# Feature projections of a linear-attention kernel as pairs of 64-row matmuls, one head on each half of the TensorE array

## The chip, the cores and the metric

The kernel runs on one core of one Trainium2 chip. The metric is the device time of one execution in microseconds. Three runs of the kernel before gave a median of 502.53 us (502.03 to 510.46).

## The reference

Eight batches of eight heads go through a linear attention, and its output through a gated convolution. Cut to what matters:

```python
def phi(x):                                   # x: (batch, head, 576, 64); w_phi: (64, 128)
    proj = np.einsum('bhsd,df->bhsf', x, w_phi)
    proj = proj - np.max(np.abs(proj), axis=-1, keepdims=True)
    return np.concatenate([np.exp(proj), np.exp(-proj)], axis=-1)
q_p, k_p = phi(q), phi(k)
kv  = np.einsum('bhsf,bhsd->bhfd', k_p, v)
num = np.einsum('bhsf,bhfd->bhsd', q_p, kv)
den = np.einsum('bhsf,bhf->bhs', q_p, k_p.sum(axis=2))[..., None] + 1e-6
x   = num / den                               # heads side by side: (batch, 576, 512)
proj = x @ w_proj                             # x1, x2, x3 of 512 columns each
y = x1 * irfft(rfft(x2) * rfft(filter)) * x3
out = y @ w_out
```

## The kernel before

**Tiles.** A batch has 576 positions, cut in five chunks of 128 (the last one has 64 real rows). Heads are worked in pairs, four pairs to a batch. For a pair, q and k are transposed on TensorE (L256, copied by ScalarE at L258 to qT and kT) so that rows 0 to 63 hold the 64 dimensions of one head and rows 64 to 127 those of the other. The weight tile wpp is 128 x 256: w_phi stands in rows 0 to 63, columns 0 to 127, and again in rows 64 to 127, columns 128 to 255; the rest is zero. One matmul over all 128 rows so projects both heads at once, and half of its products are with zeros.

**Three projection groups per pair.** `pk_group` projects k: four matmuls of 256 columns into Pk_m (two PSUM banks; chunks 0 and 1 in one, 2 and 3 in the other) and one into Pk_t for the last chunk (L272). ScalarE takes exp and exp of the negative from them (Epk, Emk, L274 to L277), VectorE the largest absolute value (mxk, L278, L281); from that come em and mxe, with which POOL (GpSimd) multiplies v (v1, v2, L292 and L296). `pqt_group` projects q with positions along the columns: two matmuls of 512 columns into Pq_m (L313), one head and one bank each, and two of 128 into Pq_t (L316); ScalarE makes Eq and Eqm (L319 to L322). `pqn_group` projects q again like k, for its largest absolute value alone (Pqn_m, Pqn_t, L335; mxq, L337, L340).

**The rest of a pair.** `kv_group` sums features times v into KV (L355); `nem_group` and `nep_group` multiply the q features with it (L373, L392), VectorE combines them (tmp L379, NEt L397), takes the reciprocal (r, L399) and writes x_nat (L404). `xt_group` transposes x_nat (xtr, L411; copied to xT at L414).

**The gated convolution of a batch** then works on xT: x2 (L598), a discrete Fourier transform as matmuls (L613), the spectrum's products on VectorE, x1 (L540) and x3 (L568), the inverse transform (L656, tail L675; the products yT at L661 and, for the tail, L680), and the last projection (L689), whose accumulator VectorE copies to o (L694), which SyncE's queue stores to memory (L695). Two o buffers alternate.

**Loads.** `load_stage` issues the loads of q, k and v of the next batch on POOL's queue, five for each tensor (L240), and four memsets on VectorE: the ones column of the v tile (L243) and the padding rows of the v, q and k tiles (L244 to L246). The memset of the ones column waits for all five loads of v, since they write the same tile.

**Order.** For each batch `merge_weighted` merges the groups of the attention of batch i with those of the convolution of batch i-1. The framework then schedules: it gives each engine its own order of instructions from the dependencies and from what it expects each instruction to take. On an engine instructions run strictly in that order. PSUM is shared by tags: "proj" has two buffers of two banks (Pk_m, Pq_m, Pqn_m, NEm, NEp), "b1" four buffers of one bank (accumulators, tails, transposes, KV).

Of the kernel before, what the change touches and what calls it, by code (L numbers as in the profile page):

```python
# [13 lines left out]
AF = mybir.ActivationFunctionType  # L14
# [3 lines left out]
PART = 128  # L18
SEQ = 576
HDIM = 64  # L20
# [3 lines left out]
NFEAT = 128  # L24
# [33 lines left out]
def psum_proj(pools, shape, name):  # L58
    return pools["psum"].tile(shape, FP32, name=name, tag="proj", bufs=PROJ_BUFS)


def psum_b1(pools, shape, dtype, name):
    return pools["psum"].tile(shape, dtype, name=name, tag="b1", bufs=B1_BUFS)
# [195 lines left out]
    return dst  # L259


def pk_group(nc, pools, cdict, st, hp, v_stage):
    wpp = cdict["wpp"]
    kT = st["kT"][hp]
    Epk = pools["attn"].tile([PART, 5, 2 * NFEAT], BF16, name="Epk", tag="Epk")
    Emk = pools["attn"].tile([PART, 5, 2 * NFEAT], BF16, name="Emk", tag="Emk")
    mxk = pools["attn"].tile([PART, 5, 2], FP32, name="mxk", tag="mxk")
    Pk_m = psum_proj(pools, [PART, 4, 2 * NFEAT], "Pk_m")
    Pk_t = psum_b1(pools, [PART, 2 * NFEAT], FP32, "Pk_t")
    for (ci, s0, rows) in s_chunks():  # L270
        dst = Pk_m[:, ci, :] if ci < 4 else Pk_t
        nc.tensor.matmul(dst, lhsT=kT[:, s0:s0 + PART], rhs=wpp,  # L272
                         start=True, stop=True)
    nc.scalar.activation(Epk[:, 0:4, :], Pk_m, AF.Exp, bias=0.0, scale=1.0)  # L274
    nc.scalar.activation(Epk[:, 4, :], Pk_t, AF.Exp, bias=0.0, scale=1.0)
    nc.scalar.activation(Emk[:, 0:4, :], Pk_m, AF.Exp, bias=0.0, scale=-1.0)  # L276
    nc.scalar.activation(Emk[:, 4, :], Pk_t, AF.Exp, bias=0.0, scale=-1.0)  # L277
    nc.vector.tensor_reduce(out=mxk[:, 0:4, :],  # L278
                            in_=Pk_m.rearrange("p c (h f) -> p c h f", h=2),
                            axis=AX.X, op=ALU.max, apply_absolute_value=True)  # L280
# [14 lines left out]
    v2 = pools["attn"].tile([PART, 2, 5, HDIM + 1], BF16, name="v2", tag="v2")  # L295
    nc.gpsimd.tensor_tensor(out=v2, in0=vsl,  # L296
                            in1=mxer.to_broadcast([PART, 2, 5, HDIM + 1]),
                            op=ALU.mult)
    st["Epk"][hp] = Epk
    st["Emk"][hp] = Emk  # L300
    st["v1"][hp] = v1
    st["v2"][hp] = v2


def pqt_group(nc, pools, cdict, st, hp):
    wpp = cdict["wpp"]
    qT = st["qT"][hp]
    Eq = pools["attn"].tile([PART, 2, 640], BF16, name="Eq", tag="Eq", bufs=3)
    Eqm = pools["attn"].tile([PART, 2, 640], BF16, name="Eqm", tag="Eqm", bufs=3)
    Pq_m = psum_proj(pools, [PART, 2, 512], "Pq_m")  # L310
    Pq_t = psum_b1(pools, [PART, 2, PART], FP32, "Pq_t")
    for j in range(2):
        nc.tensor.matmul(Pq_m[:, j, :],  # L313
                         lhsT=wpp[:, j * NFEAT:(j + 1) * NFEAT],
                         rhs=qT[:, 0:512], start=True, stop=True)
        nc.tensor.matmul(Pq_t[:, j, :],  # L316
                         lhsT=wpp[:, j * NFEAT:(j + 1) * NFEAT],
                         rhs=qT[:, 512:640], start=True, stop=True)
    nc.scalar.activation(Eq[:, :, 0:512], Pq_m, AF.Exp, bias=0.0, scale=1.0)  # L319
    nc.scalar.activation(Eq[:, :, 512:640], Pq_t, AF.Exp, bias=0.0, scale=1.0)  # L320
    nc.scalar.activation(Eqm[:, :, 0:512], Pq_m, AF.Exp, bias=0.0, scale=-1.0)  # L321
    nc.scalar.activation(Eqm[:, :, 512:640], Pq_t, AF.Exp, bias=0.0, scale=-1.0)  # L322
    st["Eq"][hp] = Eq
    st["Eqm"][hp] = Eqm


def pqn_group(nc, pools, cdict, st, hp):
    wpp = cdict["wpp"]
    qT = st["qT"][hp]
    mxq = pools["attn"].tile([PART, 5, 2], FP32, name="mxq", tag="mxq")  # L330
    Pqn_m = psum_proj(pools, [PART, 4, 2 * NFEAT], "Pqn_m")
    Pqn_t = psum_b1(pools, [PART, 2 * NFEAT], FP32, "Pqn_t")
    for (ci, s0, rows) in s_chunks():
        dst = Pqn_m[:, ci, :] if ci < 4 else Pqn_t
        nc.tensor.matmul(dst, lhsT=qT[:, s0:s0 + PART], rhs=wpp,  # L335
                         start=True, stop=True)
    nc.vector.tensor_reduce(out=mxq[:, 0:4, :],  # L337
                            in_=Pqn_m.rearrange("p c (h f) -> p c h f", h=2),
                            axis=AX.X, op=ALU.max, apply_absolute_value=True)
# [78 lines left out]
def attn_stream_groups(nc, pools, cdict, b, stages, st):  # L418
# [27 lines left out]
    def g_pk(hp):  # L446
        def f():
            pk_group(nc, pools, cdict, st, hp, v_stage)
        return f

    def g_pqt(hp):
        def f():
            pqt_group(nc, pools, cdict, st, hp)
        return f

    def g_pqn(hp):
        def f():
            pqn_group(nc, pools, cdict, st, hp)
        return f
# [395 lines left out]
```

## Time and profile before

| | |
|---|---|
| median of three runs | 502.53 us (502.03 to 510.46) |
| span of the profiled execution | 505.9 us |
| mean granted TensorE clock in it | 0.927 |
| TensorE matmuls busy | 402.8 us (80%), 3672 recorded |
| TensorE weight loads busy | 240.8 us (48%), 3734 |
| VectorE busy | 357.6 us (71%) |
| ScalarE busy | 307.3 us (61%) |
| POOL busy | 200.3 us (40%) |

The profiled execution is one of its own, beside the three timed ones; the page gives its span, from the first to the last instruction, and no other time of it. Matmul busy times overlap, since matmuls are pipelined and a row of 0.38 us can start 0.22 us after the one before it; what a matmul costs in a stream is the distance of starts. Some matmul records are missing, so a group that issues 128 may show fewer. The chain of work that ended last goes back from the last instruction to what released it, and so on; its shares say which engines and waits set the end. In a timeline row the first number is the start, the second the duration, both in microseconds, and the bracket at the end gives the engine's idle time before the row and what ended it. A row with xN merges N instructions.

### The profile page before, as it was taken

How to read it: one execution, taken by the hardware profiler on the slowest of the kernel's cores; microseconds unless marked ns; L12 is line 12 of the kernel's file. 1: busy time of each engine (PE TensorE's matmuls, PEld its weight loads, DVE VectorE, ACT ScalarE, POOL GpSimd, SP SyncE). 2: the span in 40 equal slices, each digit the busy share in tenths (PEclk: the TensorE clock that was granted, in tenths of full speed). 3: DMA queues.
4: the chain of work that ended last, by engine and by line, in shares of the span. 5: the costliest groups of instructions: out<-in, count | busy, mean ns of one | idle time of the engine just before them, and what ended most of it. 6: DMA issues, size and time to landing. Idle time of an engine off the chain costs nothing.

```text
span 505.9 us, 9253 instructions
## 1 busy us (share of the span) xinstructions
PE 402.8 (80%) x3672; PEld 240.8 (48%) x3734; DVE 357.6 (71%) x546; ACT 307.3 (61%) x611; POOL 200.3 (40%) x212
## 2 busy tenths in 40 slices
PE   1566559988688796879798795888888898889995
PEld 0344435555355553545455463554545554555442
DVE  2267654497567884697859785697777986798664
ACT  1669858877079633985189352994279636963220
POOL 9789921158012860346312760246512211221000
PEclk9856659999899998998999798998999999999999
DMA  9999970059610893039900796019910011001102
GB/s 84 176 144 95 95 47 1 0 33 78 75 54 1 53 94 89 2 21 75 124 19 1 50 75 113 1 11 74 99 53 2 2 43 53 0 2 43 53 1 95
DMA packets 119724, 26.92 MB, mean 53 GB/s; under 512 B 113472, under 2 KB 114560, under 8 KB 119680
## 3 DMA queue, kind: packets, MB, share of 16 engines
q0 software_dynamic: 114432, 16.88, 47.4%
q1 hardware_dynamic: 5248, 9.44, 5.4%
q8 instruction: 29, 0.48, 0.4%
q14 instruction: 15, 0.12, 0.1%
HBM read 33.75 MB, written 9.44 MB: 85 GB/s over the span
## 4 chain that ended last, share of the span: by engine, by line
PE 48%; DVE 20%; ACT 15%; DMA 6%; POOL 6%; issue 5%; DVEq 0%; POOLq 0%; ACTq 0%
PE acc L598 7%; PE acc L656 7%; PE acc L568 6%; DVE x_nat L404 5%; PE acc L613 5%; DMA out_dram<-o 4%; ACT Epk L274 3%; PE acc L689 3%; ACT Emk L276 3%; PE trp L256 3%; DVE mxk L278 2%; PE xtr L411 2%; PE acc L540 2%; PE KV L355 2%; DVE NEt L397 2%
## 5 line engine op out<-in xcount | busy, mean ns | idle before, releaser
L414 ACT COPY xT<-xtr 128x640 bf16<-128x640 bf16 x32 | 22.5, 702 | 78.6 <-PE xtr L411 78.6
L278 DVE TENSOR_REDUCE mxk<-Pk_m 128x8 f32<-128x1024 f32 x32 | 39.1, 1221 | 41.8 <-ACT Emk L276 41.7
L337 DVE TENSOR_REDUCE mxq<-Pqn_m 128x8 f32<-128x1024 f32 x32 | 39.0, 1218 | 14.7 <-PE Pqn_m L335 14.4
L411 PE MATMUL xtr<-ident,x_nat 128*128 128x128 bf16 x160 | 16.3, 240 | 39.9 <-DVE x_nat L404 39.9
L598 PE MATMUL acc<-wproj_sb,xT 128*128 128x512 bf16 x153 | 44.3, 411 | 3.6 <-ACT qT L258 3.3
L240 POOL DMA_DIRECT2D qs<-in_q_dram x40 | 34.5, 874 | 27.4 <-PE trp L256 20.1
L274 ACT ACTIVATE Epk<-Pk_m 128x1024 bf16<-128x1024 f32 x32 | 32.7, 1022 | 19.2 <-PE Pk_m L272 19.2
L689 PE MATMUL acc<-wout_sb,yT 128*128 128x512 bf16 x146 | 39.8, 388 | 3.4 <-DVE yT L661 2.5
L602 DVE CAST x2n<-acc 128x512 bf16<-128x512 f32 (+1 forms) x40 | 26.9, 687 | 20.2 <-PE acc L598 20.1
L694 DVE COPY o<-acc 128x512 f32<-128x512 f32 (+1 forms) x40 | 27.2, 679 | 18.9 <-DMA out_dram<-o 9.4
L240 POOL DMA_DIRECT2D ks<-in_k_dram x40 | 33.9, 878 | 10.1 <-PE trp L256 10.1
L404 DVE TENSOR_TENSOR x_nat<-NEt,r 128x640 bf16<-128x640 f32 x32 | 35.6, 1111 | 0.6
L319 ACT ACTIVATE Eq<-Pq_m 128x1024 bf16<-128x1024 f32 x32 | 34.1, 1065 | 2.9 <-PE Pq_m L313 2.9
L568 PE MATMUL acc<-xT,wproj_sb 128*128 128x512 bf16 x120 | 35.3, 421 | 0.4
L240 POOL DMA_DIRECT2D vs<-in_v_dram x40 | 34.1, 881 | 2.8 <-POOL v_518 L296 0.6
L321 ACT ACTIVATE Eqm<-Pq_m 128x1024 bf16<-128x1024 f32 x32 | 33.8, 1058 | 0.0
L411 PEld LDWEIGHTS <-x_nat 128*128 128x128 bf16 x160 | 10.9, 106 | 48.0 <-DVE x_nat L404 46.1
L540 PE MATMUL acc<-xT,wproj_sb 128*128 128x512 bf16 x121 | 31.4, 378 | 2.7 <-ACT x1s L544 2.4
L613 PE MATMUL acc<-x2n,fwdS 128*128 128x512 bf16 x117 | 29.1, 378 | 5.3 <-ACT Cxs L617 5.0
L276 ACT ACTIVATE Emk<-Pk_m 128x1024 bf16<-128x1024 f32 x32 | 33.1, 1033 | 0.0
L661 DVE TENSOR_TENSOR yT<-acc,ts 128x512 bf16<-128x512 f32 x32 | 22.0, 688 | 12.8 <-PE acc L656 7.8
L572 DVE TENSOR_TENSOR ts<-acc,x1s 128x512 bf16<-128x512 f32 x32 | 22.0, 690 | 12.1 <-PE acc L568 10.0
(315 smaller groups left out, 1066.0 us busy)
## 6 DMA issues: line engine op xcount, KB each, us to landing
out_dram<-o SPq DMA_DIRECT2D x32, 256.0 KB, 2.0
qs<-in_q_dram POOLq DMA_DIRECT2D x32, 128.0 KB, 4.1
ks<-in_k_dram POOLq DMA_DIRECT2D x32, 128.0 KB, 4.5
vs<-in_v_dram POOLq DMA_DIRECT2D x32, 128.0 KB, 4.8
wproj_sb<-in_moe_w_proj_dram POOLq DMA_DIRECT2D x4, 384.0 KB, 8.3
out_dram<-o SPq DMA_DIRECT2D x8, 128.0 KB, 2.2
qs<-in_q_dram POOLq DMA_DIRECT2D x8, 64.0 KB, 3.9
ks<-in_k_dram POOLq DMA_DIRECT2D x8, 64.0 KB, 4.2
```

Of the source, the lines that this page charges most:

```text
L240: nc.gpsimd.dma_start(out=dst[0:rows, ci, :, 0:HDIM], in_=src[b, :, s0:s0 + rows, :].rearrange("h p d -> p h d"))
L274: nc.scalar.activation(Epk[:, 0:4, :], Pk_m, AF.Exp, bias=0.0, scale=1.0)
L276: nc.scalar.activation(Emk[:, 0:4, :], Pk_m, AF.Exp, bias=0.0, scale=-1.0)
L278: nc.vector.tensor_reduce(out=mxk[:, 0:4, :], in_=Pk_m.rearrange("p c (h f) -> p c h f", h=2), axis=AX.X, op=ALU.max, apply_absolute_value ...
L337: nc.vector.tensor_reduce(out=mxq[:, 0:4, :], in_=Pqn_m.rearrange("p c (h f) -> p c h f", h=2), axis=AX.X, op=ALU.max, apply_absolute_valu ...
L404: nc.vector.tensor_tensor(out=out_view, in0=num_view, in1=r_b, op=ALU.mult)
L411: nc.tensor.transpose(trp[:, ci, :], x_nat[:, ci, t * PART:(t + 1) * PART], ident)
L540: nc.tensor.matmul(acc, lhsT=wproj[:, kt, m * PART:(m + 1) * PART], rhs=xT_sb[:, kt, 0:512], start=(kt == 0), stop=(kt == 3))
L568: nc.tensor.matmul(acc, lhsT=wproj[:, kt, 1024 + m * PART:1024 + (m + 1) * PART], rhs=xT_sb[:, kt, 0:512], start=(kt == 0), stop=(kt == 3))
L598: nc.tensor.matmul(acc, lhsT=xT_sb[:, kt, s0:s0 + PART], rhs=wproj[:, kt, 512:1024], start=(kt == 0), stop=(kt == 3))
L613: nc.tensor.matmul(acc, lhsT=mat[:, kt, m * PART:(m + 1) * PART], rhs=x2n[:, kt, :], start=(kt == 0), stop=(kt == 4))
L689: nc.tensor.matmul(acc, lhsT=yT[:, kt, s0:s0 + PART], rhs=wout[:, kt, :], start=(kt == 0), stop=(kt == 3))
```

## The change

The four 256-column matmuls of Pk_m and of Pqn_m become eight of 128 columns: for each chunk one per head, each over the 64 rows that hold this head, with that head's block of wpp. The first of a pair sits on the upper half of the array's rows, the second on the lower half. Pk_m and Pqn_m are laid out by head first, so that the two matmuls of a pair write different PSUM banks; the readers on ScalarE and VectorE take views that bring their results into the old order. The fifth chunk stays one matmul of 128 rows. In `pqt_group` the two 512-column matmuls take 64 rows each, and the two 128-column ones stay as they were, in a loop of their own.

```diff
+def row_tiled_natural(nc, P_m, P_t, xT, wpp, ci, s0):
+    if ci == 4:
+        nc.tensor.matmul(P_t, lhsT=xT[:, s0:s0 + PART], rhs=wpp,
+                         start=True, stop=True)
+        return
+    for j in range(2):
+        r0 = j * HDIM
+        nc.tensor.matmul(P_m[:, j, ci, :], lhsT=xT[r0:r0 + HDIM, s0:s0 + PART],
+                         rhs=wpp[r0:r0 + HDIM, j * NFEAT:(j + 1) * NFEAT],
+                         start=True, stop=True)
 ...
-    Pk_m = psum_proj(pools, [PART, 4, 2 * NFEAT], "Pk_m")
+    Pk_m = psum_proj(pools, [PART, 2, 4, NFEAT], "Pk_m")
 ...
     for (ci, s0, rows) in s_chunks():
-        dst = Pk_m[:, ci, :] if ci < 4 else Pk_t
-        nc.tensor.matmul(dst, lhsT=kT[:, s0:s0 + PART], rhs=wpp,
-                         start=True, stop=True)
-    nc.scalar.activation(Epk[:, 0:4, :], Pk_m, AF.Exp, bias=0.0, scale=1.0)
+        row_tiled_natural(nc, Pk_m, Pk_t, kT, wpp, ci, s0)
+    Epk_v = Epk[:, 0:4, :].rearrange("p c (h f) -> p h c f", h=2)
+    Emk_v = Emk[:, 0:4, :].rearrange("p c (h f) -> p h c f", h=2)
+    nc.scalar.activation(Epk_v, Pk_m, AF.Exp, bias=0.0, scale=1.0)
 ...
     for j in range(2):
+        r0 = j * HDIM
         nc.tensor.matmul(Pq_m[:, j, :],
-                         lhsT=wpp[:, j * NFEAT:(j + 1) * NFEAT],
-                         rhs=qT[:, 0:512], start=True, stop=True)
+                         lhsT=wpp[r0:r0 + HDIM, j * NFEAT:(j + 1) * NFEAT],
+                         rhs=qT[r0:r0 + HDIM, 0:512], start=True, stop=True)
+    for j in range(2):
         nc.tensor.matmul(Pq_t[:, j, :],
```

`pqn_group` changes as `pk_group` does. The built program changes in more than these lines, since the scheduler places the instructions anew. On TensorE there are 256 more matmuls with their weight loads, and 97 stretches of 64-row matmuls among the 128-row ones that were not there before. ScalarE's and SyncE's orders are the same. On VectorE some instructions change places; this is the place in four of the hand-overs from one batch to the next, with the lines of the kernel before:

```
before                              after
L379 tmp<-NEm,cq                    L379 tmp<-NEm,cq
L680 yT<-acct,ts                    L680 yT<-acct,ts
L694 o<-acc                         L243 memset vs (ones column)
L397 NEt<-NEp,tmp                   L694 o<-acc
L694 o<-acc                         L397 NEt<-NEp,tmp
L399 r, L379 tmp, L404 x_nat        L694 o<-acc
L694 o<-acc                         L399 r, L379 tmp, L404 x_nat
L397 NEt<-NEp,tmp                   L694 o<-acc
L694 o<-acc                         L397 NEt<-NEp,tmp
L399 r                              L694 o<-acc
L243 memset vs (ones column)        L399 r
L404 x_nat                          L244 memset vs (padding)
L529 memset yT                      L404 x_nat
L694 o<-acc (64 rows)               L694 o<-acc (64 rows)
L244 memset vs (padding)            L529 memset yT
```

In several batches the memset of x2n (L524) also moves ahead of tmp (L379), and on POOL one load of k moves ahead of two multiplications of v in the first batch.

More of the change, by code (lines that the diff above doesn't have):

```diff
@@ L267, in pk_group @@
     mxk = pools["attn"].tile([PART, 5, 2], FP32, name="mxk", tag="mxk")
-    Pk_m = psum_proj(pools, [PART, 4, 2 * NFEAT], "Pk_m")
+    Pk_m = psum_proj(pools, [PART, 2, 4, NFEAT], "Pk_m")
     Pk_t = psum_b1(pools, [PART, 2 * NFEAT], FP32, "Pk_t")
     for (ci, s0, rows) in s_chunks():
-        dst = Pk_m[:, ci, :] if ci < 4 else Pk_t
-        nc.tensor.matmul(dst, lhsT=kT[:, s0:s0 + PART], rhs=wpp,
-                         start=True, stop=True)
-    nc.scalar.activation(Epk[:, 0:4, :], Pk_m, AF.Exp, bias=0.0, scale=1.0)
+        row_tiled_natural(nc, Pk_m, Pk_t, kT, wpp, ci, s0)
+    Epk_v = Epk[:, 0:4, :].rearrange("p c (h f) -> p h c f", h=2)
+    Emk_v = Emk[:, 0:4, :].rearrange("p c (h f) -> p h c f", h=2)
+    nc.scalar.activation(Epk_v, Pk_m, AF.Exp, bias=0.0, scale=1.0)
     nc.scalar.activation(Epk[:, 4, :], Pk_t, AF.Exp, bias=0.0, scale=1.0)
-    nc.scalar.activation(Emk[:, 0:4, :], Pk_m, AF.Exp, bias=0.0, scale=-1.0)
+    nc.scalar.activation(Emk_v, Pk_m, AF.Exp, bias=0.0, scale=-1.0)
     nc.scalar.activation(Emk[:, 4, :], Pk_t, AF.Exp, bias=0.0, scale=-1.0)
-    nc.vector.tensor_reduce(out=mxk[:, 0:4, :],
-                            in_=Pk_m.rearrange("p c (h f) -> p c h f", h=2),
+    nc.vector.tensor_reduce(out=mxk[:, 0:4, :].rearrange("p c h -> p h c"),
+                            in_=Pk_m,
                             axis=AX.X, op=ALU.max, apply_absolute_value=True)
@@ L330, in pqn_group @@
     mxq = pools["attn"].tile([PART, 5, 2], FP32, name="mxq", tag="mxq")
-    Pqn_m = psum_proj(pools, [PART, 4, 2 * NFEAT], "Pqn_m")
+    Pqn_m = psum_proj(pools, [PART, 2, 4, NFEAT], "Pqn_m")
     Pqn_t = psum_b1(pools, [PART, 2 * NFEAT], FP32, "Pqn_t")
     for (ci, s0, rows) in s_chunks():
[L334 to L338, printed above, removed]
+        row_tiled_natural(nc, Pqn_m, Pqn_t, qT, wpp, ci, s0)
+    nc.vector.tensor_reduce(out=mxq[:, 0:4, :].rearrange("p c h -> p h c"),
+                            in_=Pqn_m,
                             axis=AX.X, op=ALU.max, apply_absolute_value=True)
```

## The prediction

> **What bounds the kernel now.** The page comes first: the span, then the chain that ended last, by engine and by line.
>
> ```profile
> span 505.9 us, 9253 instructions
> ## 4 chain that ended last, share of the span: by engine, by line
> PE 48%; DVE 20%; ACT 15%; DMA 6%; POOL 6%; issue 5%; DVEq 0%; POOLq 0%; ACTq 0%
> L411 PE MATMUL xtr<-ident,x_nat 128*128 128x128 bf16 x160 | 16.3, 240 | 39.9 <-DVE x_nat L404 39.9
> ```
>
> No engine is the bound for the whole span. PE carries 48% of the chain, and its largest idle time, 39.9 us, is ended by VectorE's x_nat (L404). So I read the chain in order of time where one batch hands over to the next.
>
> ```profile
> 242.99 0.63 PE KV L355 x20
> ...
> 246.58 3.59 DMA out_dram<-o
> ...
> 251.79 0.84 DVE x_nat L404
> ...
> 253.40 0.89 PE acc L598 x4
> ```
>
> The next batch's first projection (L598) needs the last x_nat, so whatever delays VectorE here delays PE, and everything behind it. This is VectorE's timeline there, from the tail product yT<-acct (L680) on:
>
> ```profile
> 243.58 0.41 DVE L680 TENSOR_TENSOR yT<-acct,ts 128x256 bf16<-128x256 f32 x1
> 244.52 0.69 DVE L694 COPY o<-acc 128x512 f32<-128x512 f32 x1 [0.53 <-PE acc L689]
> ...
> 249.60 0.69 DVE L694 COPY o<-acc 128x512 f32<-128x512 f32 x1 [1.50 <-DMA out_dram<-o]
> ...
> 251.79 0.83 DVE L404 TENSOR_TENSOR x_nat<-NEt,r 128x640 bf16<-128x640 f32 x1
> 251.85 0.09 DVE L243 MEMSET vs<- 128x40 bf16 x1
> ...
> 253.46 0.49 DVE L244 MEMSET vs<- 64x520 bf16 x1 [0.17 <-DVE o L694]
> ```
>
> Remember the 0.09 us memset of vs (L243). It writes the ones column of the next batch's v tile and waits for all five loads of that tile. In this order it stands near the end and waits for little.
>
> **Part 1: the pairs on PE.** A group Pk or Pqn has four 256-column matmuls, which become eight of 128 columns and 64 rows; Pq has two of 512, which become two of 64 rows. What a change of row size costs is shown before the change by L203, whose fifth transpose has 64 rows:
>
> ```profile
> 118.50 0.35 PE L203 MATMUL ptr<-ident,fwdS 128*128 128x128 bf16 x2
> 118.65 0.20 PE L203 MATMUL ptr<-ident,fwdS 64*128 64x64 bf16 x1
> 118.78 0.23 PE L316 MATMUL Pq_t<-qT,wpp 128*128 128x128 bf16 x1
> 119.58 0.45 PE L411 MATMUL xtr<-ident,x_nat 128*128 128x128 bf16 x5
> 257.92 0.38 PE L313 MATMUL Pq_m<-qT,wpp 128*128 128x512 bf16 x1
> 258.14 0.22 PE L316 MATMUL Pq_t<-qT,wpp 128*128 128x128 bf16 x1
> 271.80 0.61 PE L272 MATMUL Pk_m<-wpp,kT 128*128 128x256 bf16 x4
> 272.25 0.27 PE L272 MATMUL Pk_t<-wpp,kT 128*128 128x256 bf16 x1
> ```
>
> The first row merges two transposes: the last of 128 rows, which starts at 118.50, and the one of 64 rows, which the second row shows alone, from 118.65. Five plain transposes take 0.45 with a last one of about 0.23, so they start 0.055 apart. Into the 64-row form therefore costs 0.15 - 0.055 = 0.095 us. Out of it, 118.65 to 118.78 is 0.13, where the small matmuls of the KV row start 0.63 / 20 = 0.032 apart: 0.10 us. One excursion costs 0.195 us.
>
> What it earns: four Pk matmuls take 272.25 - 271.80 = 0.45 us. If the halves run side by side, eight small ones go at the fastest pace that the trace shows, 0.032 each, 0.25 us: a gain of 0.20. A Pq matmul takes 258.14 - 257.92 = 0.22; two become 0.22 + 0.03, a gain of 0.19. If the halves don't overlap, eight of 0.055 take 0.44 and nothing is gained. The scheduler splits a few groups, and the built program has 97 excursions. Side by side: 97 x (0.195 - 0.20) = about -1 us of PE time. One after the other: 97 x 0.19 = 18.4 us of PE time, of which the 48% that PE holds of the chain is 8.8 us. The other end, all gain and no switch because PE waits there anyway, is 97 x -0.2 x 0.48 = -9.3 us. I take **0**: no row shows two halves at once, but the gain cancels with the switch that the rows do show.
>
> The Trainium skill has a rule against this change: "TensorEngine Tiling (Array Packing)", section Tiling Modes, Key Properties, says that changing the tiling mode drains TensorE, while different tiles run in parallel. By the drain alone the sum is +8.8 us, by both statements it is about 0. This trace agrees on the drain, about 0.1 us each way, and no run so far shows the parallel part.
>
> The evictions (L274, L276, L278, L337) keep their element counts and read whole banks; only write order changes. Their groups:
>
> ```profile
> L274 ACT ACTIVATE Epk<-Pk_m 128x1024 bf16<-128x1024 f32 x32 | 32.7, 1022 | 19.2 <-PE Pk_m L272 19.2
> L319 ACT ACTIVATE Eq<-Pq_m 128x1024 bf16<-128x1024 f32 x32 | 34.1, 1065 | 2.9 <-PE Pq_m L313 2.9
> ```
>
> Eq, which writes two separate pieces, is the nearest: 0.043 us more, on 64 activations 2.8 us of ACT, 15% of the chain, 0.4 us. I cost it at 0.
>
> **Part 2: the order on VectorE.** The diff doesn't touch load_stage, but the scheduler places instructions by what it expects of PE, and the order of the built program differs. In four hand-overs (near 186, 245, 302 and 361 us) the memset L243 moves from behind the fourth o copy to directly behind yT<-acct, ahead of all o, NEt and x_nat work. VectorE works in order, so all of these now queue behind five v loads. When the last of those is issued, and when VectorE gets there:
>
> ```profile
> 186.46 0.72 POOL L240 DMA_DIRECT2D vs<-in_v_dram  x1
> 244.81 0.72 POOL L240 DMA_DIRECT2D vs<-in_v_dram  x1
> 302.04 0.72 POOL L240 DMA_DIRECT2D vs<-in_v_dram  x1
> 360.80 0.72 POOL L240 DMA_DIRECT2D vs<-in_v_dram  x1
> 184.90 0.41 DVE L680 TENSOR_TENSOR yT<-acct,ts 128x256 bf16<-128x256 f32 x1
> 300.47 0.41 DVE L680 TENSOR_TENSOR yT<-acct,ts 128x256 bf16<-128x256 f32 x1
> 359.57 0.41 DVE L680 TENSOR_TENSOR yT<-acct,ts 128x256 bf16<-128x256 f32 x1
> vs<-in_v_dram POOLq DMA_DIRECT2D x8, 64.0 KB, 5.0
> ```
>
> The tail chunk (64 KB) lands 5.0 us after its issue. So the four landings are 191.46, 249.81, 307.04 and 365.80, while VectorE is free at 185.31, 243.99, 300.88 and 359.98: it stands still for 6.15, 5.82, 6.16 and 5.82 us, together 24.0.
>
> Part of that is idle already, because the o buffers wait for output DMAs that share the engines with the v loads:
>
> ```profile
> 191.74 0.69 DVE L694 COPY o<-acc 128x512 f32<-128x512 f32 x1 [2.32 <-PE acc L689]
> 193.92 0.69 DVE L694 COPY o<-acc 128x512 f32<-128x512 f32 x1 [0.75 <-DMA out_dram<-o]
> 308.51 0.69 DVE L694 COPY o<-acc 128x512 f32<-128x512 f32 x1 [3.51 <-DMA out_dram<-o]
> 365.50 0.69 DVE L694 COPY o<-acc 128x512 f32<-128x512 f32 x1 [1.41 <-PE acc L689]
> ```
>
> With the v loads landed first, outputs no longer collide and these gaps can close. With the 0.53 before the first o (taken as the same in all four) they are 3.60, 2.03, 4.04 and 1.94, together 11.6 us. Left are 24.0 - 11.6 = 12.4 us. The large memset L244 (0.49) also moves ahead of the last x_nat; less some overlap, about 0.4 x 4 = 1.6. **Sum 14.0 us**, all ahead of L598 on the chain. Nothing covers it: PE's instructions behind xtr wait for x_nat. Bounds: 25.6 if no gap closes; with the row's shortest landing for v loads, 3.5 us, 6 less, so 8.
>
> **Part 3: the clock.** PE now waits longer in these places. Two windows right after hand-overs, and the wait of PE before one:
>
> ```profile
> 195.66 0.45 PE L411 MATMUL xtr<-ident,x_nat 128*128 128x128 bf16 x5 [4.00 <-DVE x_nat L404]
> 252.67 0.45 PE L411 MATMUL xtr<-ident,x_nat 128*128 128x128 bf16 x5 [2.33 <-DVE x_nat L404]
> 196.00:200.00 4.00, 4.00 (x21) 1.97 (x19) 1.46 (x3) 1.98 (x3) 0.00 (x0) 0.57 0.19 48
> 253.00:257.00 4.00, 4.00 (x34) 2.29 (x32) 2.18 (x5) 2.97 (x5) 0.00 (x0) 1.00 0.20 54
> ```
>
> After 4.00 us of waiting the granted clock was 0.57 over the next 4 us, after 2.33 us it was 1.00; in the cold window PE is busy throughout and loses 0.43 x 4 = 1.7 us. With longer waits the hand-overs near 245 and 361 can turn cold too: 0 to 3.4 us. I take **1.7**, the middle. The Trainium skill, "TensorE: Matmul & The Clock Gate", Part 1, says that about 3.4 us without activity halves the clock; the two rows agree.
>
> Small moves: in several batches the memset of x2n and tmp change places, and both still stand ahead of the products with Sxs; one k load goes ahead of two POOL multiplications in the first batch, once the 0.72 of an issue above. Both at 0.
>
> **Sum**: 0 + 14.0 + 1.7 = 15.7 us. The profiled execution is no basis for a total: its span alone is 3.4 us over the median of 502.5, and the page gives no time outside the span. The difference is added to that median: **518 us**, +3.1%. About 2% is what a measurement of this kernel can tell from no change.
>
> **The rivals.** *Halves one after the other*: the same stalls and 8.8 us of switches, 527 us. For it: the switch is in the rows, the overlap isn't. Against: by the diff the two halves of a pair read different rows and write different PSUM banks.
>
> *Pairs pay in full*: PE waits ahead of many Pk groups (ACT's kT copies) and hides the switch: 518 - 9.3 = 509. Against: Pk_t and the next L540 or L598 stand right behind the group and take the second switch.
>
> *Stall absent, not slower*: the v loads are over before VectorE arrives. The place is POOL's queue, where they follow the last multiplication by em; they would have to be issued 5.8 us earlier against VectorE than in the rows. Price: all 15.7 us gone, 502.5, or down to 493 if the pairs also pay. Against: nothing in the change shortens that queue by more than 0.2 us. A part of the same: if the landings shrink by 1.5 us, 512.
>
> **How the numbers follow.** Forecast 0.63 (511 to 523), halves in series 0.15, pairs pay 0.12, stall absent 0.10. Over 512.6 us lie nearly all of the first two: slower 0.76. Within 2%: the third, half of the fourth and the forecast's edge, 0.19. Faster, below 492.5: only no stall and paying pairs, 0.05. The range 508 to 528 holds the first three and leaves out the fourth and the far bounds.
>
> **What would show it.** Right: in four hand-overs VectorE idles about 6 us with v loads as the releaser, ahead of the memset of vs; output DMAs land in about 2 us there; x_nat's wait on PE grows by about 3 us each; Pk's pairs start 0.03 apart with a 0.1 us gap on either side. Wrong: the memset finds its loads landed, or pairs start 0.055 apart (series), or Pk groups of 0.25 us without gaps (pairs pay). The forecast falls if the v loads land much earlier, or if later waits in the batch swallow the delay.

## The result and the profile after

| | before | after |
|---|---|---|
| median (range) | 505.73 us (502.03 to 510.46, 4 runs) | 531.96 us (528.44 to 534.61, 4 runs) |
| ratio to before, 95% interval | | 1.0531 (1.0424 to 1.0637) |
| time and span of the profiled execution | span 505.9 us | 530.72 us, span 528.9 us |
| mean granted TensorE clock in it | 0.927 | 0.906 |

The change makes the kernel 5.3% slower. The forecast was 518 us, 3.1% slower, with a range of 508 to 528. The direction and the mechanism were right, the size was too small, and the time lies outside the range. Of the 14 us between forecast and time, 3.2 come from the base: with a fourth run the median of before is 505.7 and not 502.5. The change itself costs 26.2 us by the medians and 23.0 by the spans of one profiled execution each, where the forecast had 15.7. The 3.2 us between these two differences are not explained by any trace; single executions of the kernel before lie up to 8 us apart.

These are the lines of the page after that answer to those of before: span, chain, and three groups. The changed kernel's lines are 12 higher behind the new helper (o is L706, xtr L423, Epk L286); pairs are issued from L269.

```profile
span 528.9 us, 9773 instructions
...
PE 38%; DVE 20%; ACT 16%; DMA 9%; POOL 9%; issue 8%; DVEq 0%; POOLq 0%; ACTq 0%
...
L706 DVE COPY o<-acc 128x512 f32<-128x512 f32 (+1 forms) x40 | 27.3, 685 | 39.8 <-DMA vs<-in_v_dram 27.3
...
L423 PE MATMUL xtr<-ident,x_nat 128*128 128x128 bf16 x160 | 17.6, 254 | 33.6 <-DVE x_nat L416 33.6
L286 ACT ACTIVATE Epk<-Pk_m 128x1024 bf16<-128x1024 f32 x32 | 32.8, 1024 | 16.1 <-PE Pk_m L269 16.0
```

The copy o<-acc now has 39.8 us of idle time ahead of it, and 27.3 us of that is ended by loads of v, which o doesn't read. An instruction shown as waiting for something it doesn't use stands behind one that does: here the memset of the ones column. PE's share of the chain fell from 48% to 38%. Epk's eviction is as long as before (1024 ns beside 1022).

VectorE's timeline in the second of the four hand-overs, in the kernel after:

```profile
244.36 0.42 DVE L692 TENSOR_TENSOR yT<-acct,ts 128x256 bf16<-128x256 f32 x1
251.01 0.69 DVE L706 COPY o<-acc 128x512 f32<-128x512 f32 x1 [6.24 <-DMA vs<-in_v_dram]
251.09 0.09 DVE L243 MEMSET vs<- 128x40 bf16 x1
...
257.11 0.69 DVE L706 COPY o<-acc 128x512 f32<-128x512 f32 x1 [1.17 <-PE acc L701]
257.72 0.21 DVE L411 RECIPROCAL r<-NEt 128x10 f32<-128x10 f32 x1
258.09 0.49 DVE L244 MEMSET vs<- 64x520 bf16 x1 [0.17 <-issue]
258.61 0.82 DVE L416 TENSOR_TENSOR x_nat<-NEt,r 128x640 bf16<-128x640 f32 x1
```

After yT<-acct VectorE stands still for 6.24 us until the loads of v have landed. (The profile shows the copy just ahead of the memset and hangs the wait on it; in the program the memset comes first.) Then comes an idle time that the forecast didn't have, 1.17 us for the accumulator of the last projection, and ahead of x_nat the large memset with its full 0.49 us.

The four hand-overs in one table for each kernel, from the end of yT<-acct to the end of the last x_nat of the batch. The columns are the stretch, its length, busy time (and instructions) of PE, PEld, DVE, ACT and POOL, the granted clock, the DMA share and GB/s. Before:

```profile
185.30:195.60 10.30, 5.26 (x52) 2.81 (x52) 6.67 (x14) 0.80 (x2) 1.88 (x3) 1.00 1.05 134
244.00:252.60 8.60, 5.25 (x52) 2.81 (x51) 6.55 (x13) 0.78 (x2) 1.54 (x2) 1.00 1.18 154
300.90:311.50 10.60, 5.24 (x52) 2.81 (x51) 6.54 (x13) 0.77 (x2) 1.87 (x3) 1.00 1.06 131
360.00:368.50 8.50, 5.24 (x52) 2.81 (x51) 6.54 (x13) 0.77 (x2) 1.52 (x2) 1.00 1.16 154
sum 38.00, PE 21.00 PEld 11.24 DVE 26.30 ACT 3.12 POOL 6.80; mean PE 5.25 PEld 2.81 DVE 6.57 ACT 0.78 POOL 1.70
```

After:

```profile
183.20:198.00 14.80, 7.41 (x52) 3.60 (x51) 7.08 (x14) 0.75 (x2) 1.75 (x3) 0.77 0.73 105
244.80:259.40 14.60, 7.42 (x52) 3.60 (x51) 7.02 (x14) 0.76 (x2) 1.43 (x2) 0.77 0.72 104
308.10:323.20 15.10, 7.42 (x52) 3.61 (x51) 7.07 (x14) 0.77 (x2) 1.77 (x3) 0.67 0.74 104
373.10:389.60 16.50, 7.26 (x52) 3.60 (x51) 7.08 (x14) 0.78 (x2) 1.44 (x2) 0.69 0.67 93
sum 61.00, PE 29.51 PEld 14.41 DVE 28.25 ACT 3.06 POOL 6.39; mean PE 7.38 PEld 3.60 DVE 7.06 ACT 0.76 POOL 1.60
```

The sums differ by 61.0 - 38.0 = 23.0 us, and the spans by 528.9 - 505.9 = 23.0 us. In these two profiles the four stretches hold the whole difference. (Outside them small differences cancel: ahead of the first of them 2.1 us less than before, in the batch behind the last one 1.9 more.) The same 52 matmuls are busy for 7.4 us instead of 5.25, at a granted clock of 0.67 to 0.77 instead of 1.00: while VectorE stands still, PE waits too, and its clock falls. The first row is an accumulator's four matmuls in the second of them before; then PE's timeline there after, and the same place in the chain in order of time (start, length, what):

```profile
244.62 1.02 PE L689 MATMUL acc<-wout_sb,yT 128*128 128x512 bf16 x4
```

```profile
252.50 0.71 PE L404 MATMUL NEp<-KVs,Eq 128*128 128x65 bf16 x10 [4.90 <-DVE NEt L409]
...
255.16 1.91 PE L701 MATMUL acc<-wout_sb,yT 128*128 128x512 bf16 x4
```

```profile
245.50 5.29 DMA vs<-in_v_dram
...
255.37 1.72 PE acc L701 x4
257.09 0.02 issue
257.11 0.69 DVE o L706
```

PE waits 4.90 us for NEt, which stands behind the memset on VectorE. Then the four matmuls of an accumulator hold the chain for 1.72 us, 0.43 each, where at full clock matmuls of 512 columns follow each other after 0.22; and o waits for them. In PE's rows the four take 1.91 us, where they took 1.02 before.

What lies between the hand-overs is as long as it was. For the four stretches from the last x_nat of one batch to yT<-acct of the next, the sum row, before and then after:

```profile
sum 190.60, PE 168.92 PEld 103.30 DVE 147.75 ACT 137.08 POOL 88.52; mean PE 42.23 PEld 25.82 DVE 36.94 ACT 34.27 POOL 22.13
```

```profile
sum 190.80, PE 168.56 PEld 95.70 DVE 146.03 ACT 137.34 POOL 88.92; mean PE 42.14 PEld 23.93 DVE 36.51 ACT 34.34 POOL 22.23
```

And one whole batch late in the kernel, at a granted clock of 1.00 throughout and without loads, before and after:

```profile
419.40:470.20 50.80, 45.00 (x450) 27.48 (x458) 41.72 (x60) 34.94 (x71) 11.54 (x8) 1.00 0.07 23
```

```profile
442.40:493.20 50.80, 45.01 (x483) 25.58 (x490) 41.56 (x60) 34.99 (x71) 11.55 (x8) 1.00 0.07 25
```

With 64-row pairs in it the batch takes 50.80 us, as without them. That is the forecast's zero for the pairs, in an undisturbed batch. The batch just ahead of it is not undisturbed: 50.90 us at a clock of 1.00 before, 52.80 at 0.97 after. A group of pairs in PE's timeline after:

```profile
261.89 0.38 PE L610 MATMUL acc<-wproj_sb,xT 128*128 128x512 bf16 x1
...
262.20 0.40 PE L269 MATMUL Pk_m<-wpp,kT 64*128 64x128 bf16 x8
262.53 0.28 PE L264 MATMUL Pk_t<-wpp,kT 128*128 128x256 bf16 x1
```

From the matmul of 512 columns to the first pair 0.31 us pass, where 0.22 is the distance without a change of row size; eight small matmuls and the way out take 262.53 - 262.20 = 0.33 us, where four large ones took 0.45 (0.44 as a median over all groups at full clock). The single records show how: the two halves of a pair start 0.003 to 0.004 us apart, pairs follow each other after 0.056 to 0.066, and the last pair stands 0.15 ahead of the tail, of which 0.09 is the way out.

### The profile page after: what moved, and what is told of

It reads as the page before. It is cut to its first block, busy times and chain, and to the rows that moved or that the text cites. A ratio compares the mean times of both kernels' runs of the same rounds, so it can differ in the third digit from the quotient of the medians.

```text
span 528.9 us, 9773 instructions
## 1 busy us (share of the span) xinstructions
PE 406.9 (77%) x3936; PEld 228.3 (43%) x3990; DVE 360.2 (68%) x546; ACT 307.8 (58%) x611; POOL 200.4 (38%) x212
## 4 chain that ended last, share of the span: by engine, by line
PE 38%; DVE 20%; ACT 16%; DMA 9%; POOL 9%; issue 8%; DVEq 0%; POOLq 0%; ACTq 0%
PE acc L580 6%; DMA vs<-in_v_dram 6%; PE acc L625 6%; PE acc L668 5%; DVE x_nat L416 5%; PE acc L610 5%; POOL vs L240 4%; ACT Epk L286 3%; PE trp L256 2%; PE xtr L423 2%; PE acc L701 2%; DVE NEt L409 2%; DMA out_dram<-o 2%; DVE mxk L290 2%; DVE tmp L391 2%
## 5 line engine op out<-in xcount | busy, mean ns | idle before, releaser
L304 POOL TENSOR_TENSOR v<-vs,em 128x650 bf16<-128x650 bf16 x32 | 42.3, 1322 | 236.5 <-ACT em L297 107.9
L706 DVE COPY o<-acc 128x512 f32<-128x512 f32 (+1 forms) x40 | 27.3, 685 | 39.8 <-DMA vs<-in_v_dram 27.3
L701 PE MATMUL acc<-wout_sb,yT 128*128 128x512 bf16 x146 | 44.7, 426 | 3.7 <-DVE yT L673 2.3
L308 POOL TENSOR_TENSOR v<-vs,mxe 128x650 bf16<-128x650 bf16 x32 | 47.0, 1470 | 0.0
L240 POOL DMA_DIRECT2D qs<-in_q_dram x40 | 34.5, 874 | 27.3 <-PE trp L256 26.9
L610 PE MATMUL acc<-wproj_sb,xT 128*128 128x512 bf16 x153 | 42.0, 393 | 3.0 <-ACT qT L258 2.7
L423 PE MATMUL xtr<-ident,x_nat 128*128 128x128 bf16 x160 | 17.6, 254 | 33.6 <-DVE x_nat L416 33.6
L286 ACT ACTIVATE Epk<-Pk_m 128x1024 bf16<-128x1024 f32 x32 | 32.8, 1024 | 16.1 <-PE Pk_m L269 16.0
L580 PE MATMUL acc<-xT,wproj_sb 128*128 128x512 bf16 x120 | 36.4, 440 | 0.9 <-issue 0.7
L404 PE MATMUL NEp<-KVs,Eq 128*128 128x65 bf16 x320 | 16.7, 204 | 22.0 <-DVE NEt L409 22.0
L552 PE MATMUL acc<-xT,wproj_sb 128*128 128x512 bf16 x121 | 31.5, 378 | 2.6 <-ACT x1s L556 2.2
```

The source lines that it names most:

```text
L240: nc.gpsimd.dma_start(out=dst[0:rows, ci, :, 0:HDIM], in_=src[b, :, s0:s0 + rows, :].rearrange("h p d -> p h d"))
L286: nc.scalar.activation(Epk_v, Pk_m, AF.Exp, bias=0.0, scale=1.0)
L304: nc.gpsimd.tensor_tensor(out=v1, in0=vsl, in1=emr.to_broadcast([PART, 2, 5, HDIM + 1]), op=ALU.mult)
L308: nc.gpsimd.tensor_tensor(out=v2, in0=vsl, in1=mxer.to_broadcast([PART, 2, 5, HDIM + 1]), op=ALU.mult)
L580: nc.tensor.matmul(acc, lhsT=wproj[:, kt, 1024 + m * PART:1024 + (m + 1) * PART], rhs=xT_sb[:, kt, 0:512], start=(kt == 0), stop=(kt == 3))
L610: nc.tensor.matmul(acc, lhsT=xT_sb[:, kt, s0:s0 + PART], rhs=wproj[:, kt, 512:1024], start=(kt == 0), stop=(kt == 3))
```

## The experiments

Two theories stood at the start. **The memset's place**: the scheduler's move of the ones column ahead of o, NEt and x_nat makes the whole loss, whatever PE does. **The pairs**: 64-row matmuls lose time themselves, by switches or because TensorE's clock falls more often. All ratios are against the kernel before on the same chip, with 95% intervals.

**The memset early, without pairs.** The full-row kernel, with load_stage issued ahead of the first last-projection group of iterations 2 to 5 instead of after all groups, and the first o copy ordered behind the memset. The other engines keep their orders.

```diff
-                g()
+                if (2 <= i <= 5 and stages[i + 2] is None
+                        and "g_final" in g.__qualname__):
+                    stages[i + 2] = load_stage(nc, pools, q, k, v, i + 2)
+                    with tc.issue_after(pools["ones"]):
+                        g()
+                else:
+                    g()
```

> The matmuls are those of the kernel before, all of 128 rows; every engine's order is that of before, but in four hand-overs the two memsets of the next v tile stand directly behind the tail product yT<-acct and around the first o copy, as in the changed kernel. Theory 'the wait' (the loss is VectorE standing still for the v loads): 21 to 26 us slower than before, VectorE idle about 6 us four times with the v loads as the releaser. Rival 'the pairs' (the loss is the drains of the 64-row matmuls, and the stall only fills time that would be lost anyway): within 3 us of before.

Measured: 533.82 us, ratio 1.0539 (1.0469 to 1.0610). Its wait of o on v loads, and the hand-over near 247 us in VectorE's timeline:

```profile
DVE o L694 <- DMA vs<-in_v_dram: 25.1, 4, 7.4
```

```profile
247.46 0.41 DVE L680 TENSOR_TENSOR yT<-acct,ts 128x256 bf16<-128x256 f32 x1
253.71 0.69 DVE L694 COPY o<-acc 128x512 f32<-128x512 f32 x1 [5.83 <-DMA vs<-in_v_dram]
253.78 0.09 DVE L243 MEMSET vs<- 128x40 bf16 x1
```

The same four waits, 25.1 us beside 27.3, and the same loss, without a single 64-row projection. The memsets' place alone is enough. (The padding memset L244 stands ahead of the second o copy here, and ahead of x_nat in the changed kernel; its 0.49 us lie ahead of x_nat in both.)

**The memset late, with pairs.** The changed kernel, the memset ordered behind the last reciprocal for the batches that had stalled.

```diff
-    nc.vector.memset(vs[:, :, :, HDIM:HDIM + 1], 1.0)
+    with (pools["tc"].issue_after(pools["last_r"]) if b >= 4 else ExitStack()):
+        nc.vector.memset(vs[:, :, :, HDIM:HDIM + 1], 1.0)
```

> All pairs of the changed kernel, but the memset of the ones column is held behind the last reciprocal of each hand-over, its place in the kernel before. Theory 'the wait': back to the time of before, between -2 and +2 us of it. Rival 'the pairs': at least 20 us slower than before.

Measured: ratio 1.0093 (1.0030 to 1.0157). The largest wait of o is now that for its own output transfers:

```profile
DVE o L707 <- DMA out_dram<-o: 9.9, 8, 2.1
```

So 4.4 of the 5.3% go with the memset's place, and about 0.9% (0.3 to 1.6) stay with the pairs; by the medians, 509.19 us beside 507.90, it is 0.3%. This is where the forecast's zero comes into question.

**Fixed v tiles, with and without pairs.** Two v tiles that live through the kernel, whose ones and padding are written once, so that no memset of v waits for a load at all; on the changed kernel and on the kernel before.

```diff
-    vs = stage.tile([PART, 5, NHEADS, HDIM + 1], BF16, name="vs", tag="vs")
+    vs = pools["vs_fixed"][b % 2]
...
-    nc.vector.memset(vs[:, :, :, HDIM:HDIM + 1], 1.0)
-    nc.vector.memset(vs[64:128, 4, :, :], 0.0)
```

> All pairs, and two fixed v tiles whose ones column and padding are written once at the start, so that no memset of v waits for a load in any batch. Theory 'the wait': -4 to +1 us against before, since four hand-overs also lose a 0.5 us memset. Rival 'the pairs': at least 20 us slower than before.

> Full-row matmuls of the kernel before with the two fixed v tiles. It is the partner of the run with pairs and fixed tiles: the difference of the two is what the pairs do alone. Theory 'the wait': 0 to -3 us against before, and within 3 us of its partner (97 stretches, each about 0.01 us shorter on TensorE). Rival 'the pairs': over 15 us faster than its partner.

Measured: pairs 1.0010 (0.9967 to 1.0052), full rows 0.9920 (0.9875 to 0.9964). With the memsets gone both gain 0.8% by the ratios (1.0093 to 1.0010, and 1 to 0.9920), and the distance between them stays 0.9%. By the medians (509.19 to 508.78 us, and 507.90 to 503.71) the pairs gain only 0.1%, and the distance is 1.0%: the distance is the firmer of the two.

**The layout alone.** The kernel with fixed tiles and pairs, but each small matmul over all 128 rows. Layout, views, split matmuls and every engine's order are those of the pairs; no row size changes.

```diff
-        nc.tensor.matmul(P_m[:, j, ci, :], lhsT=xT[r0:r0 + HDIM, s0:s0 + PART],
-                         rhs=wpp[r0:r0 + HDIM, j * NFEAT:(j + 1) * NFEAT],
+        nc.tensor.matmul(P_m[:, j, ci, :], lhsT=xT[:, s0:s0 + PART],
+                         rhs=wpp[:, j * NFEAT:(j + 1) * NFEAT],
```

> The kernel with pairs and fixed v tiles, but each of the small matmuls runs over all 128 rows (the half of wpp's column block that belongs to the other head is zero): the layout by head, the views of the readers, the number of matmuls and every engine's order stay, the 64-row form and its switches go. The pairs with fixed v tiles took 4.6 us more than full-row matmuls with fixed v tiles (ratios 1.001 and 0.992). Theory 'the array' (what is left comes from the 64-row form: switches, or a clock that is granted less): ratio 0.99 to 0.995 against before. Rival 'the layout' (the views, or the changed places of tmp and x2n's memset): ratio 1.00, like the pairs.

Measured: 0.9944 (0.9900 to 0.9988), between full rows and pairs, nearer to full rows, as 'the array' expected. It was measured a second time:

> A repetition of the layout without the 64-row form on the chip of the two runs beside it, with two o buffers: it ties them to the earlier runs. Expected 0.990 to 0.998 against before, and a mid-batch cold window in no more batches than the full-row kernel has.

Measured: 0.9997 (0.9960 to 1.0034), over the range expected here and beside the pairs, as 'the layout' expected. Two measurements of one kernel differ by 0.5%, so the question needed all three kernels side by side; that follows below.

**Halves in series.** The kernel with fixed tiles and pairs, with the four matmuls of one head ahead of the four of the other.

```diff
-    for (ci, s0, rows) in s_chunks():
-        row_tiled_natural(nc, Pk_m, Pk_t, kT, wpp, ci, s0)
+    for (ci, s0, j) in [(c, c * PART, j) for j in range(2) for c in range(4)] + [(4, 512, 0)]:
+        row_tiled_natural(nc, Pk_m, Pk_t, kT, wpp, ci, s0, j)
```

> Pairs and fixed v tiles, but the four matmuls of one head's rows come first and then the four of the other's, in Pk and Pqn, so that neighbours sit on the same half of the array; every engine's order of work is the same. Theory 'side by side': starts 0.056 us apart instead of 0.003 within a pair, a group 0.2 us longer, 64 groups 13 us of TensorE time and with its 48% of the chain about 6 us more than the pairs with fixed tiles: ratio 1.01 to 1.02. Rival 'it doesn't matter' (TensorE waits around these groups anyway): ratio 1.00.

Measured: 1.0016 (0.9978 to 1.0054), the ratio of the pairs. A group in its PE timeline:

```profile
264.01 0.41 PE L266 MATMUL Pk_m<-wpp,kT 64*128 64x128 bf16 x8
264.35 0.28 PE L262 MATMUL Pk_t<-wpp,kT 128*128 128x256 bf16 x1
```

0.34 us from the first to the tail, where eight matmuls 0.056 apart and the way out would take about 0.54. The records start at 264.006, .019, .071, .085, .127, .141, .183 and .196: two streams, 0.013 to 0.014 apart, each with its own 0.056 or so. The built program issues the four matmuls of one head ahead of the four of the other, so the second stream is most simply the other half, which starts without waiting for the first half's remaining three. The records don't name the head, so this is read from the spacing and not shown; if it is so, starts on the two halves need not keep the program's order. The experiment didn't do what it was made for: nothing was put in series, and it says nothing on what a series would cost. Its time also stands beside that of the layout alone, taken with it: 1.0016 against 0.9944, 0.7% for the 64-row form.

**Three o buffers.** Where no memset stalls, o waits for its output transfers most. The same two kernels with a third buffer.

```diff
-            o = mp.tile([PART, 512], FP32, name="o", tag="onat", bufs=2)
+            o = mp.tile([PART, 512], FP32, name="o", tag="onat", bufs=3)
```

> Full-row matmuls, fixed v tiles, and three output buffers o instead of two, so that a copy to o waits less for an output transfer that collides with the loads. The four hand-overs of before hold 11.6 us of such idle time on VectorE. If the chain runs through it, 4 to 10 us less than before: ratio 0.975 to 0.99. If PE or the transposes of x_nat end last there anyway: 0.99, as without the third buffer.

> The same with the pairs. Theory 'the array': 3 to 6 us over the run with full-row matmuls and three o buffers, so 0.985 to 1.00 against before. Rival: no difference between the two.

Measured: full rows 0.9768 (0.9711 to 0.9825), 499.1 us; pairs 0.9880 (0.9826 to 0.9934), 503.5 us. The wait of o for its transfers with full rows, with two buffers and with three:

```profile
DVE o L692 <- DMA out_dram<-o: 11.8, 8, 3.3
```

```profile
DVE o L692 <- DMA out_dram<-o: 5.8, 5, 3.1
```

Full rows with fixed v tiles and three o buffers beat both kernels of the study. The distance to the pairs is 1.1%.

**Pairs in three of four head pairs.** The kernel with pairs, fixed tiles and three o buffers, but Pq and Pqn of one head pair over all 128 rows: of the third, where the granted clock had halved near 166 us in the profile with pairs and not in that without, and, to compare, of the first.

```diff
+        rw = slice(0, PART) if hp == 2 else slice(r0, r0 + HDIM)
-                         lhsT=wpp[r0:r0 + HDIM, j * NFEAT:(j + 1) * NFEAT],
-                         rhs=qT[r0:r0 + HDIM, 0:512], start=True, stop=True)
+                         lhsT=wpp[rw, j * NFEAT:(j + 1) * NFEAT],
+                         rhs=qT[rw, 0:512], start=True, stop=True)
```

> Pairs, fixed v tiles and three o buffers, but the q projections of head pair 2 (Pq_m and Pqn_m), which stand right ahead of TensorE's 1.5 us wait in the middle of a batch, run over all 128 rows; the order on every engine stays. Theory 'the clock' (pairs make TensorE less active, a window of 3.4 us falls under the mark and the clock halves): the cold windows in the middle of the batches from 135 and 362 us go, as in the full-row kernel, and most of the loss against it returns: 2 to 4 us less than pairs everywhere (0.988), ratio 0.979 to 0.984. Rival 'the switches' (each stretch costs the same): 16 of 97 stretches go, a sixth of the 5 us: 0.986 to 0.988.

> The same edit for head pair 0 instead of 2, whose q projections stand at the start of a batch, where TensorE is busy. Theory 'the clock': the cold windows in the middle of a batch stay and the time stays near that of pairs everywhere, ratio 0.986 to 0.990. Rival 'the switches': 21 of 97 stretches go, about 1 us: 0.985 to 0.988, no higher than with pair 2 in full rows.

Measured: 0.9871 (0.9813 to 0.9928) and 0.9851 (0.9814 to 0.9888). They differ neither from each other nor from the 0.9880 with all pairs. The stretch in question, with pairs everywhere and then with the third head pair over all rows (columns as in the windows above, the third from the end is the granted clock):

```profile
166.80:170.30 3.50, 2.86 (x11) 1.57 (x13) 1.66 (x3) 0.69 (x1) 3.50 (x4) 0.50 0.55 34
```

```profile
166.80:170.30 3.50, 3.50 (x28) 1.73 (x26) 2.72 (x6) 0.98 (x3) 3.50 (x6) 1.00 0.68 43
```

There the clock did stay at 1.00 instead of 0.50. In the profiles this batch went from 57.80 to 53.40 us, and the next three grew by 3.3 us together; the measured time did not follow beyond its interval of 0.6%. So a stretch at half clock makes its own batch longer, but taking one particular stretch away moves others and does not return the loss.

**Full rows, layout, pairs, side by side.** Three kernels with fixed v tiles and three o buffers, timed side by side. The diffs are those above.

> Full rows, fixed v tiles, three o buffers, as e7, on one chip beside the two kernels that follow. All theories: the ratio of e7, 0.977 (0.971 to 0.983). It is the base of the comparison: the pairs with the same tiles stood at 0.988 beside e7.

> Fixed v tiles, three o buffers, the head-first layout, the views and the small matmuls of the changed kernel, but each over all 128 rows (the half of the other head multiplies zeros); every engine has the order of e8. Row size theory (64-row matmuls cost about 5 us, by the clock or by switches): the time of full rows, 0.975 to 0.980. Layout theory (views, split matmuls and the changed places of tmp and x2n cost it): the time of the pairs, 0.986 to 0.990. In between, 0.980 to 0.986: both have a share.

> Pairs, fixed v tiles, three o buffers, as e8. All theories: the ratio of e8, 0.988 (0.983 to 0.993), 1.1% over full rows. Should the distance to full rows be under 0.4% here, the cost of the pairs alone seen so far was chance.

Measured: full rows 0.9760 (0.9711 to 0.9808), 497.3 us; layout 0.9836 (0.9784 to 0.9887), 501.8 us; pairs 0.9867 (0.9824 to 0.9910), 502.9 us. The distance from full rows to pairs is there a third time: 0.9% with two o buffers, 1.1 and 1.1% with three, so it isn't chance. By the medians of this comparison 4.5 of the 5.6 us come with the layout and 1.1 with the row size. The intervals of layout and pairs overlap widely, those of layout and full rows by a little (0.9784 and 0.9808). The runs with two o buffers don't settle it: of the two with the layout alone, 0.9997 stands with the pairs (1.0010), but 0.9944 stands near full rows (0.9920) and 0.7% under the 64-row kernel measured beside it (1.0016). So it is shown that the changed matmuls, layout and order together cost about 1%; how much of it the layout brings and how much the row size is open.

Where the time is, batch by batch (from the last x_nat of one batch to that of the next; columns as above). Full rows:

```profile
134.30:188.50 54.20, 46.38 (x462) 28.04 (x462) 43.04 (x64) 35.04 (x71) 24.30 (x23) 1.00 0.60 60
...
301.20:359.00 57.80, 50.01 (x458) 29.79 (x458) 43.28 (x63) 35.06 (x71) 23.68 (x23) 0.92 0.55 53
...
410.40:461.70 51.30, 45.43 (x458) 27.44 (x458) 41.83 (x61) 34.95 (x71) 11.55 (x8) 1.00 0.07 22
sum 327.40, PE 282.32 PEld 169.35 DVE 256.94 ACT 210.21 POOL 118.46; mean PE 47.05 PEld 28.23 DVE 42.82 ACT 35.03 POOL 19.74
```

The layout alone:

```profile
303.70:363.10 59.40, 49.84 (x490) 30.27 (x490) 43.09 (x63) 35.08 (x71) 23.69 (x23) 0.90 0.54 51
363.10:417.00 53.90, 48.05 (x490) 29.61 (x490) 41.71 (x60) 35.09 (x71) 11.55 (x8) 0.95 0.07 24
417.00:468.40 51.40, 45.50 (x490) 28.05 (x490) 41.79 (x61) 34.96 (x71) 11.55 (x8) 1.00 0.07 24
sum 332.30, PE 287.10 PEld 175.10 DVE 256.28 ACT 210.34 POOL 118.49; mean PE 47.85 PEld 29.18 DVE 42.71 ACT 35.06 POOL 19.75
```

Pairs:

```profile
135.60:193.60 58.00, 50.67 (x494) 27.98 (x494) 43.03 (x64) 35.20 (x71) 24.31 (x23) 0.92 0.55 55
...
418.30:469.70 51.40, 45.38 (x490) 25.51 (x490) 41.76 (x62) 34.99 (x71) 11.55 (x8) 1.00 0.07 24
sum 334.10, PE 288.10 PEld 160.28 DVE 256.27 ACT 210.58 POOL 118.48; mean PE 48.02 PEld 26.71 DVE 42.71 ACT 35.10 POOL 19.75
```

At full clock a batch takes 51.30, 51.40 and 51.40 us, with PE busy for 45.43, 45.50 and 45.38: neither layout nor row size costs more than 0.1 us there. Over six batches the spans differ by 4.9 us (layout) and 6.7 us (pairs) from full rows, and PE's busy time by 4.8 and 5.8, while VectorE and ScalarE stay the same. From the lengths and granted clocks of all six rows the clock is halved for about 21, 31 and 33 us (an estimate), and 10 to 12 us more at half clock lose about 5 to 6. So in these profiles the extra time of the six batches is matmuls that run longer at the halved clock, and hardly longer waits. The first of the six is the plainest case: 54.20 us at 1.00 with full rows, 58.00 us at 0.92 with pairs. Not all of the distance lies there: the whole spans differ by 6.8 and 8.0 us, and the batch ahead of the six takes 62.70, 64.20 and 65.00 us at 0.97, 0.98 and 0.95, so that the layout loses 1.5 us in it without a lower clock.

What stays open is why the clock halves more often with the new layout and its order. Which stretches go cold (run at half clock) changes from kernel to kernel. That the change of layout and order shifts waits by a few tenths of a microsecond, and so decides which stretches go cold, is a guess that no run here tests.

## Why the prediction was wrong, step by step

**Part 1, the pairs at 0: right at full clock.** The switch measured 0.09 us in (0.31 for 0.22) and 0.09 to 0.10 out, the forecast had 0.095 and 0.10. The eight small matmuls of a Pk group take 0.24 us without the way out, 0.20 less than before, where the forecast had 0.20; about 0.01 us a group are left, 1 us over 97 excursions; the forecast's own product, 97 x 0.005, is 0.5. The halves run side by side, so *halves one after the other* falls, and *pairs pay in full* falls too: the switches are paid in most groups. (Some Pqn groups end in a wait of PE of 0.7 us or more, which hides the way out.) The evictions cost nothing (1024 ns for 1022). What the part missed is the 0.9 to 1.1% that the pairs cost once the stall is gone, some 5 us; in the profiles most of it goes with the granted clock, and whether layout or row size brings it is open. In the changed kernel's time this cost can't be told: the early memset alone gives 1.0539 and the change 1.0531, though intervals of 0.7 and 1.1% on either side would let it hide.

**Part 2, the order on VectorE at 14.0: the right mechanism, the failed size.** The hand-overs cost 23.0 us (23.1 by the sum of the terms), where this part had 14.0. The terms of the sum, as measured:

| term | forecast | measured |
|---|---|---|
| waits for the v loads | 24.0 | 27.3 |
| idle times of before that close | -11.6 | -11.6 + 4.7 + 0.7 |
| memset L244 ahead of x_nat | 1.6 | 2.0 |
| sum | 14.0 | 23.1 |

The waits are 6.38, 6.24, 6.67 and 8.06 us in place of 6.15, 5.82, 6.16 and 5.82. The last load landed 5.1, 5.3, 5.4 and 7.0 us after its issue, where the forecast took the median of 5.0 for all four, and some 0.2 to 0.3 us pass from the landing to the copy. Only the fourth is far off, and why its load took 7.0 isn't known.

The step that failed most is "these gaps can close". The old waits did close: the outputs of 128 rows land 2.0 us after their issue there, where before the first two of each hand-over took 3.6 to 6.3. (The two rows of before that name PE's accumulator, 2.32 and 1.41 us, were such waits too: the transfers issued at 186.56 and 361.23 landed 5.1 and 4.2 us later, just ahead of the copies at 191.74 and 365.50.) But the fourth o copy now waits for PE's accumulator in every hand-over, 1.17 us each, 4.7 in all, and 0.17 us of issue stand ahead of the memset L244, 0.7 in all. The accumulator is late because PE runs at half clock: its four matmuls take 1.72 us instead of about 0.9, and its first one starts 0.51 us behind the start of the transposes ahead of it instead of 0.29, together about 1.0 of the 1.17. I had two separate terms for the stall and for the clock; they are one. The stall stops PE, the clock falls behind the stop (in the second hand-over it is 1.00 up to 250.0 us and 0.50 from 252.5 to 257.0, with PE idle from 247.6 to 252.5), and the halved clock makes most of the wait behind it.

**Part 3, the clock at 1.7: right that it falls, wrong place.** It was put into the stretches after the hand-overs, which cost nothing more than before (190.6 and 190.8 us). The clock fell inside the hand-overs, to 0.67 to 0.77, and is paid there, by the 4.7 us above. The prediction's rows showed 0.57 after 4.00 us of waiting of PE; a wait of 6 us of VectorE in mid hand-over should have been read by the same rows.

**The bounds.** The far bound of Part 2, 25.6 with no gap closing, was close to the 23.0 that came, but by chance: the old gaps closed, and new ones of 5.4 us opened beside longer waits. The range left it out as a far end; the trace of before gave no reason to favour full closing over none, and half of it, 5.8, would have given 524 us.

**The rival "stall absent"** was wrong for the change, but the two experiments that take the stall out show its price: 4.4% by the memset's place alone, and 5.2% with fixed tiles (1.0531 to 1.0010), of which fixed tiles also gain 0.8% by the ratios where nothing stalls.

## What to carry to other kernels

A change of matmul shapes can cost through an instruction that it doesn't touch: compare each engine's order in the two built programs, and look first for memsets and small writes into tiles that are being loaded, since on an engine that works in order they put everything behind them into the load's wait. Write constant parts of a loaded tile once, in a tile that lives through the kernel, and that wait does not arise. And when a stall on another engine stops TensorE for some microseconds, price the stall and the matmuls at half clock behind it as one thing.

## What was not expected of the hardware

- Two halves of the array seem to take their 64-row matmuls as two streams, by the spacing of the starts. In program order one half after the other, two starts still lay 0.013 us apart, and the group took 0.34 us, where with heads alternating in program order it took 0.33.
- A stretch of 64-row pairs pays about 0.19 us for going in and out, and four pairs of 128 columns gain 0.20 us over full rows: break-even at about four pairs. The Trainium skill, "TensorEngine Tiling (Array Packing)", Tiling Modes, Key Properties, says that changing the mode drains TensorE and that tiles run in parallel; this trace agrees with both, with 0.09 us each way and 0.003 to 0.004 us between the starts of a pair.
- Over six batches, PE's busy time differed by 4.8 to 5.8 us between kernels whose batches at full clock are equal to 0.1 us. Most of a difference of 1% between two kernels can go with the granted clock.
- The mean granted clock of a whole execution does not rank the kernels. With three o buffers, three of the six executions with pairs had 0.969 to 0.973 and took 502.2 to 503.1 us, while the six with full rows had 0.927 to 0.948 and took 496.2 to 499.9. The start of the kernel weighs much in that mean: it takes 70.5 us at 1.00 in the profile with the first head pair over all rows, and 71.6 us at 0.81 in that with full rows.
